# Opening of a retention-plus-FFN kernel: four overlapped steps fed by 512-byte rows, in place of four serial blocks fed by 256-byte rows

## The chip, the cores and the metric

The kernel runs on one core of a Trainium2 chip. The metric is the device time in microseconds (us) of one execution. Most figures below are medians over several executions; single executions are named as such. The time of an execution is about 1.7 us longer than the span that its profile shows.

PE is the matmul engine (TensorE), PEld its weight loads, DVE is VectorE, ACT is ScalarE, POOL is GpSimd, SP issues DMAs. A name with q (SPq) is the queue of that engine. PSUM is the memory that PE writes its results to. "FFN" is the bilinear feed-forward part.

## The reference, cut to what matters

```python
def _attn_ref(q, k, v):                      # q, k, v: float32 [8, 8, 576, 64]
    scores = scale * np.matmul(q, k.transpose(0, 1, 3, 2))
    gamma = 1.0 - 2.0 ** (-5.0 - np.arange(H))
    Dmat = np.where(rel >= 0, gamma[:, None, None] ** rel, 0.0)   # causal decay
    return np.matmul(scores * Dmat, v)

def reference(...):
    x = attn_out.transpose(0, 2, 1, 3).reshape(4608, 512)
    return (x @ w_a) * (x @ w_b) @ w_out     # 512 -> 1536 -> 512
```

The FFN is nearly all of the matmul work. The kernel computes attention for the tokens just ahead of the FFN that consumes them. At the start no token is ready, so there is an opening: the first 512 tokens go through attention before the first FFN matmul can run. Only this opening changes.

## The kernel before

The decay is split into a factor of the key's position (folded into v) and one of the query's position (a table `qs`, applied when an output is scaled). Loads of the opening are 128 tokens each, with one 256-byte row per token and head:

```python
    def load(i):
        tiles = []
        for name, src in (("qf", q), ("kf", k), ("vf", v)):
            t = half_of(stage, i, [DM], FP32, name)
            for r0, n, b, s0 in rows_of(i):
                nc.sync.dma_start(
                    t[r0:r0 + n, :].rearrange("p (h d) -> p h d", h=H),
                    src[b, :, s0:s0 + n, :].rearrange("h s d -> s h d"))
            tiles.append(t)
        staged[i] = tiles
```

The opening is four blocks of 128 tokens in order, each one cast, transposed, scored, masked, multiplied with v and the running state, and scaled. `warm` issues filler matmuls on the identity, whose results nobody reads; fourteen of them stand in the opening:

```python
    def warm(count):
        w = ps_ffn.tile([128, 4, 128], FP32, tag="ab", name="w")
        for _ in range(count):
            nc.tensor.matmul(w, identity,
                             identity.unsqueeze(1).to_broadcast([128, 4, 128]),
                             start=True, stop=True)
    ...
    idle = {0: (0, 0), 1: (0, 3), 2: (2, 4), 3: (1, 4)}
    ...
    cast(0, "dve")
    transposes(0)
    ...
    for i in range(4):
        if idle[i][0]:
            warm(idle[i][0])
        scores(i)
        flush()                      # the masks, on DVE
        if i == 2:
            load_w(0, W1)            # FFN weights, issued from POOL
            load_w(W1, W2)
        if i < 3:
            cast(i + 1, "dve" if i == 2 else "act")
        state(i)
        if idle[i][1]:
            warm(idle[i][1])
        if i < 3:
            transposes(i + 1)
            outputs(i)
            flush()                  # the scaling, on DVE
    ...
    outputs(3, halves=True)
    flush()
```

## Time and profile before

| kernel before | value |
|---|---|
| median of 3 runs | 336.48 us (336.28 to 336.54) |
| span of the profiled run | 335.1 us |
| PE busy | 95% |
| first FFN matmul | 21.74 us |

These are lines of the page of the kernel before: busy time of each engine, the DMA queues, the engines' shares in the chain of work that ended last, and one group of FFN matmuls (count, busy us, mean ns of one).

```profile
PE 318.8 (95%) x3422; PEld 165.8 (49%) x3458; DVE 164.4 (49%) x307; ACT 124.7 (37%) x261; POOL 112.4 (34%) x139
...
q1 hardware_dynamic: 147440, 45.10, 69.1%
...
PE 92%; DVE 2%; DMA 2%; issue 1%; SPq 1%; ACT 1%; POOL 0%; ACTq 0%; DVEq 0%
...
L607 PE MATMUL pb<-xT,wb_sb 128*128 128x512 bf16 (+1 forms) x474 | 111.1, 357 | 0.5
```

PE is what the kernel waits for nearly everywhere, so the place to win something is where PE has no useful work: before 21.74 us. The chain of work in order of time (start, us, what) shows why the opening is as long as it is:

```profile
4.02 5.11 DMA kf<-in_k_dram
9.13 0.05 issue
9.18 0.62 POOL qkb L254
...
12.12 1.28 PE w L651 x3
13.40 0.85 PE tp L269 x8
...
16.16 1.29 DVE sT L322 x2
17.45 0.34 DVE qkb L252
...
19.79 0.86 PE w L651 x4
20.65 0.34 PE o L341 x8
20.99 0.24 PE o L349 x8
21.24 0.02 issue
21.26 0.44 DVE xT L356
21.70 0.04 issue
21.74 0.38 PE pa L592
```

First comes a wait for a load (until 9.13 us), then PE itself, fillers included, then masks and scalings on DVE between short PE batches. `tp` are transposes, `sT` the masked scores, `o` the outputs, `xT` the scaled outputs that the FFN reads, `w` the fillers, `pa` the first FFN matmul.

The clock is part of this. The trace holds a record of each stretch with its granted clock. In the kernel before the first record, a grant of the full clock, comes at 15.2 us. Ahead of it the clock is at half, as the chain above shows: three fillers take 1.28 us at 12.12 us (0.43 us each), and four take 0.86 us at 19.79 us (0.215 us each). From then on it is full to the end. One thing has to be known of the mean clock that each run lists: a stretch ahead of the first record does not count in it, so this run is listed at 1.0 in spite of 15 us at half clock.

### The profile page before, as it was taken

How to read it: one execution, taken by the hardware profiler on the slowest of the kernel's cores; microseconds unless marked ns; L12 is line 12 of the kernel's file. 1: busy time of each engine (PE TensorE's matmuls, PEld its weight loads, DVE VectorE, ACT ScalarE, POOL GpSimd, SP SyncE). 2: the span in 40 equal slices, each digit the busy share in tenths (PEclk: the TensorE clock that was granted, in tenths of full speed). 3: DMA queues.
4: the chain of work that ended last, by engine and by line, in shares of the span. 5: the costliest groups of instructions: out<-in, count | busy, mean ns of one | idle time of the engine just before them, and what ended most of it. 6: DMA issues, size and time to landing. Idle time of an engine off the chain costs nothing.

```text
span 335.1 us, 8277 instructions
## 1 busy us (share of the span) xinstructions
PE 318.8 (95%) x3422; PEld 165.8 (49%) x3458; DVE 164.4 (49%) x307; ACT 124.7 (37%) x261; POOL 112.4 (34%) x139
## 2 busy tenths in 40 slices
PE   2989999999999999999999999999999999999995
PEld 1544445857744454545454545454545454444443
DVE  3546346565746366476237623753475347414321
ACT  8544423442624343253225232523342334213321
POOL 4570016952428638375243603370330000000000
PEclk9999999999999999999999999999999999999999
DMA  9999999989999999999599249974960420020002
GB/s 169 210 179 208 210 197 210 252 199 216 172 176 226 200 209 246 205 185 184 147 225 196 65 138 196 184 118 128 216 99 3 125 65 2 3 94 31 0 33 94
DMA packets 152230, 50.35 MB, mean 150 GB/s; under 512 B 142848, under 2 KB 147712, under 8 KB 152192
## 3 DMA queue, kind: packets, MB, share of 16 engines
q1 hardware_dynamic: 147440, 45.10, 69.1%
q0 software_dynamic: 4752, 4.72, 8.8%
q8 instruction: 27, 0.44, 0.6%
q14 instruction: 11, 0.09, 0.1%
HBM read 37.75 MB, written 9.44 MB: 141 GB/s over the span
## 4 chain that ended last, share of the span: by engine, by line
PE 92%; DVE 2%; DMA 2%; issue 1%; SPq 1%; ACT 1%; POOL 0%; ACTq 0%; DVEq 0%
PE pa L592 28%; PE pb L607 28%; PE po L627 27%; DMA kf<-in_k_dram 2%; PE o L525 2%; PE o L538 1%; PE sc L499 1%; PE kv L448 1%; SPq L121 1%; PE w L651 1%; PE tp L269 1%; DVE sT L322 1%; PE sc L316 1%; PE o L349 1%; PE o L341 0%
## 5 line engine op out<-in xcount | busy, mean ns | idle before, releaser
L612 DVE TENSOR_TENSOR hT<-ha,pb 128x512 bf16<-128x512 bf16 (+1 forms) x120 | 75.8, 633 | 98.4 <-PE pb L607 86.8
L600 ACT CAST ha<-pa 128x512 bf16<-128x512 f32 (+1 forms) x120 | 65.0, 543 | 126.6 <-PE pa L592 124.8
L592 PE MATMUL pa<-xT,wa_sb 128*128 128x512 bf16 (+1 forms) x464 | 109.5, 357 | 2.7 <-DVE xT L356 1.1
L607 PE MATMUL pb<-xT,wb_sb 128*128 128x512 bf16 (+1 forms) x474 | 111.1, 357 | 0.5
L627 PE MATMUL po<-wo_sb,hT 128*128 128x512 bf16 (+1 forms) x430 | 95.2, 373 | 1.6 <-issue 1.3
L607 PEld LDWEIGHTS <-wb_sb 128*128 128x128 bf16 x480 | 46.9, 98 | 47.6 <-issue 1.1
L592 PEld LDWEIGHTS <-wa_sb 128*128 128x128 bf16 x480 | 45.9, 98 | 47.6 <-issue 2.4
L627 PEld LDWEIGHTS <-hT 128*128 128x128 bf16 x444 | 42.4, 98 | 47.0
L388 POOL CAST qkb<-qf 64x1024 bf16<-64x1024 f32 x15 | 15.4, 1030 | 84.0 <-DMA qf<-in_q_dram 71.5
L638 DVE COPY osb<-po 128x512 f32<-128x512 f32 (+1 forms) x18 | 12.2, 676 | 43.2 <-PE po L627 43.2
L393 POOL TENSOR_TENSOR vb<-vf,vs 128x1024 bf16<-128x1024 f32 x15 | 28.5, 1902 | 7.3 <-PE o L538 2.1
L636 ACT COPY osb<-po 128x512 f32<-128x512 f32 (+1 forms) x19 | 10.9, 575 | 49.0 <-PE po L627 46.1
L547 DVE TENSOR_TENSOR xT<-o,qs 128x512 bf16<-128x512 f32 x30 | 19.6, 681 | 5.3 <-PE o L538 5.3
L467 DVE TENSOR_TENSOR sums<-kv,sums 128x256 f32<-128x256 f32 x47 | 19.8, 422 | 4.6 <-PE kv L448 3.1
L508 DVE TENSOR_TENSOR sT<-sc,mask 128x512 bf16<-128x512 f32 x30 | 19.7, 679 | 0.0
L388 POOL CAST qkb<-kf 64x1024 bf16<-64x1024 f32 x15 | 15.5, 1034 | 7.2 <-DMA kf<-in_k_dram 6.8
L392 POOL CAST qkb<-kf 64x512 bf16<-64x512 f32 x30 | 17.6, 614 | 0.9
L392 POOL CAST qkb<-qf 64x512 bf16<-64x512 f32 x30 | 17.6, 614 | 0.6
L479 ACT CAST states<-sums 64x512 bf16<-64x512 f32 (+1 forms) x30 | 17.2, 574 | 0.4
L255 POOL TENSOR_TENSOR vb<-vf,vs 128x512 bf16<-128x512 f32 x6 | 6.3, 1047 | 30.1 <-DMA vf<-in_v_dram 30.1
L269 PE MATMUL tp<-identity,qkb 128*128 128x128 bf16 x48 | 5.6, 265 | 6.4 <-ACT qkb L250 5.4
L322 DVE TENSOR_TENSOR sT<-sc,mask 128x512 bf16<-128x512 f32 x12 | 7.7, 685 | 2.4 <-PE sc L316 2.4
(71 smaller groups left out, 142.9 us busy)
## 6 DMA issues: line engine op xcount, KB each, us to landing
out_dram<-osb SPq DMA_DIRECT2D x35, 256.0 KB, 2.2
qf<-in_q_dram SPq DMA_DIRECT2D x32, 256.0 KB, 4.9
kf<-in_k_dram SPq DMA_DIRECT2D x32, 256.0 KB, 5.3
vf<-in_v_dram SPq DMA_DIRECT2D x32, 256.0 KB, 5.0
wo_sb<-in_moe_w_out_dram POOLq DMA_DIRECT2D x3, 512.0 KB, 18.3
qf<-in_q_dram SPq DMA_DIRECT2D x8, 128.0 KB, 5.1
kf<-in_k_dram SPq DMA_DIRECT2D x8, 128.0 KB, 5.5
vf<-in_v_dram SPq DMA_DIRECT2D x8, 128.0 KB, 4.8
```

The source lines that it names most:

```text
L388: nc.gpsimd.tensor_copy(qkb[0:64, w], t[0:64])
L392: nc.gpsimd.tensor_copy(to[:, :, 1 - r], fro[:, :, r])
L393: nc.gpsimd.tensor_tensor(vb.rearrange("p (k h d) -> p k h d", k=2, h=H), vf.rearrange("p (k h d) -> p k h d", k=2, h=H), vs2[:, n % BL].u ...
L467: nc.vector.tensor_tensor(sums[:, i], own, prev, op=ALU.add)
L479: nc.scalar.copy(into[half(1 - r)].rearrange("p (k a) c d -> p a k (c d)", a=2)[:, 1, which.start // 2: which.stop // 2], sums[half(r)].re ...
L508: nc.vector.tensor_tensor(sT[:, on].rearrange("p c k s -> p (c k) s"), sc[:, on].rearrange("p c k s -> p (c k) s"), mask3.unsqueeze(1).to_ ...
L547: nc.vector.tensor_tensor(x_of(t0, 128).rearrange("p c (a s) -> p c a s", a=2), o[:, :, :, kp].rearrange("p a c s -> p c a s"), qs[:, :, s ...
L592: nc.tensor.matmul(pa[:, 0:n], wa_sb[:, c, fs], xT[:, c], start=(c == 0), stop=(c == NC - 1))
L600: nc.scalar.copy(ha[:, 0:n], pa[:, 0:n])
L607: nc.tensor.matmul(pb[:, 0:n], wb_sb[:, c, fs], xT[:, c], start=(c == 0), stop=(c == NC - 1))
L612: nc.vector.tensor_tensor(hT[:, F, 0:n], has[F][:, 0:n], pb[:, 0:n], op=ALU.mult)
L627: nc.tensor.matmul(po[:, 0:width], hT[:, F, u * 128:(u + 1) * 128], wo_sb[:, F, cols], start=(F == 0), stop=(F == NF - 1))
```

## The change

The intent: load rows that are 512 bytes long (two neighbouring tokens of one head lie side by side in memory), which makes even and odd tokens two interleaved halves ("parity order"); cut the opening into four steps of 256 tokens by four heads instead of four blocks of 128 tokens by eight heads; and place each step's casts, transposes and scores ahead of the outputs of the step in front, so that the engines overlap. The core of the diff:

```diff
+    def load_step(n, hh, which):
+        ...
+        nc.sync.dma_start(
+            paired[n][which][:, hh * DM:(hh + 1) * DM]
+            .rearrange("p (h e) -> p h e", h=4),
+            (q, k, v)[which][0, 4 * hh:4 * hh + 4, 256 * n:256 * n + 256, :]
+            .rearrange("h (p two) d -> p h (two d)", two=2))
+
+    STEPS = [(0, 0), (1, 0), (0, 1), (1, 1)]
...    cut: score_step, state_step and output_step, in 64x64 quarters of PE
-    idle = {0: (0, 0), 1: (0, 3), 2: (2, 4), 3: (1, 4)}
...
+    warm(3)
+    score_step(0)
+    transpose_step(1, 0, "act")
+    transpose_step(1, 1, "act")
+    ...
+    cast_step(2, 1, "pool")
+    warm(2)
+    state_step(0, (0, 1))
+    score_step(1)
+    cast_step(2, 0, "act")
+    output_step(0)
+    state_step(1, (0,))
+    transpose_step(2, 0, "act")
+    transpose_step(2, 1, "dve")
+    load_w(0, W1)
+    output_step(1)
+    ...
+    score_step(2)
+    ...
+    transpose_step(3, 0, "act")
+    transpose_step(3, 1, "act")
+    state_step(2, (0, 1))
+    ...
+    score_step(3)
+    output_step(2)
+    state_step(3, (0,))
+    output_step(3)
+    for i in (1, 3):
+        state_step(i, (1,))
```

Five fillers are left of fourteen. The first FFN block stores its rows in two DMAs (even and odd tokens), and the query table of 768 columns is made again during that block in the usual token order.

## The prediction

> What bounds it now. The page gives PE 95% busy over the 335.1 us span; the chain that ended last is 92% PE, nearly all feed-forward (FFN) matmuls, which the change leaves alone. Only the opening is at stake. In the critical chain the first FFN matmuls that need the second half of the opening's outputs start at 22.17 us; from there to the end (313 us) I expect no change. Before them the chain is first loads (the second block's keys land at 9.13 us), then PE work at the cold clock (12 to 15.7 us), then scores, mask, output, scaling in series: mask 1.29 us for two instructions, scaling 0.69, PE batches 0.4.
>
> Loads. The q/k/v loads use 256-byte packets. The trace's packets show 217 GB/s from 2 to 16.4 us: one per 18.9 ns on each of 16 engines, 1.2 us for a 256 KB load. The weights (float32 read, bf16 written) show 206 GB/s written, so 412 GB/s read: the engines can do more. The Trainium skill ("DMA: Bandwidth & Descriptors", Specifications) puts line rate at 512 bytes or more; this trace has no such load yet. Estimate from both rates: 0.65 to 0.85 us per 256 KB load, so the loads end near 12 us instead of 16.4, and weights are issued near 10 us instead of 15.0. DMA stops being what the opening waits for.
>
> What then bounds it: ScalarE and the score, mask, output ping-pong. ScalarE carries four exponentials (914 ns for 640 columns, so about 0.75 for 512) until 5.9 us, ahead of its first transpose copy; then copies and casts of 0.59 to 0.61 us and state copies of 0.27 to 0.37. VectorE: four masks of about 1.3, four scalings of 0.69, casts and copies of 0.42. Walking both queues in order with these durations (estimates): first scores 7.3 us (before 7.15; three cold fillers stand ahead of them), mask 0 until 9.2, mask 1 11.7, scaling 0 12.4, scaling 1 13.7, mask 2 15.0, last transpose copy on ScalarE 15.3, mask 3 17.2, scaling 2 17.9, output 3 waits for that (one PSUM buffer), scaling 3 19.1. FFN matmuls of the second half then start at 19.2, against 22.17: 3.0 us saved.
>
> Costs added: total bytes are the same; the first block's stores split in two (hidden); ScalarE makes tables of 768 instead of 128 columns during the first FFN block (3 us more on an engine 37% busy, hidden); some 120 more small matmuls, in the opening's idle time.
>
> Predicted: 336.5 - 3.0 = 333.4 us, 80% range 331.6 to 335.2. Faster by over 2% 0.05, within 2% 0.94, slower 0.01.
>
> What would show each step: 512-byte packets at 300 to 400 GB/s and loads done by about 12 us; the first full FFN matmuls near 19 us; ScalarE nearly without gaps from 9 to 16 us; more PE idle in the opening; FFN from its start to the end still 313 us.
>
> What could make it wrong. The clock: the Trainium skill ("TensorE: Matmul & The Clock Gate", Part 1) says the array runs at half rate until a window of sustained activity; the trace agrees (four transposes take 0.61 us before 15.5 us, 0.40 after). The change has five fillers instead of fourteen; if FFN starts cold, up to 1.7 us come back. Weights issued early may slow the last loads (1 us). If 512-byte packets are no faster, the gain shrinks to 2 us. If copies overlap better than I walked them, up to 4.5 us are saved.

## The result

| | median | lowest to highest | runs |
|---|---|---|---|
| before | 336.51 us | 336.28 to 336.75 | 4 |
| after | 335.26 us | 334.64 to 668.54 | 4 |

The ratio is 0.9957 (95% interval 0.9937 to 0.9976). Ratios here are the mean time of one kernel's fast runs over that of the other's of the same rounds, so not quite the ratio of the medians. The three fast runs of after are 334.64, 335.10 and 335.43 us. The fourth, the profiled one, took 668.54 us, twice as long. It is a slow run and does not enter the ratio; it does enter the listed median.

The predicted 333.4 us was too low, and the listed median of 335.26 lies just outside the predicted range (331.6 to 335.2). The median of the three fast runs alone, 335.10, lies just inside it. But they save about 1.5 us where 3.1 were forecast, so less than half.

The first page of after is of that slow run. Its busy times and the group that answers to the FFN group above:

```profile
PE 648.1 (97%) x3545; PEld 247.6 (37%) x3581; DVE 166.9 (25%) x303; ACT 129.7 (19%) x271; POOL 113.1 (17%) x146
...
L768 PE MATMUL pb<-xT,wb_sb 128*128 128x512 bf16 (+1 forms) x474 | 224.0, 632 | 1.8 <-issue 1.8
```

DVE, ACT and POOL are busy for about as long as before; only PE is slower, and its three groups of FFN matmuls in about the same proportion (each is busy for 2.0 to 2.1 times as long). Its trace holds no clock record at all: the full clock was never granted in 667 us (below it is called the stuck run). This is not what the change does to a normal run, but it says where to look.

A second run of the same kernel (after_again, below) gave a profile 332.6 us long and with the clock granted at 9.5 us and then never taken back. It answers to the page of before:

```profile
PE 317.5 (95%) x3545; PEld 165.5 (50%) x3581; DVE 165.7 (50%) x303; ACT 128.9 (39%) x271; POOL 113.6 (34%) x146
...
q1 hardware_dynamic: 141360, 45.10, 66.6%
...
PE 93%; DVE 3%; issue 2%; ACT 2%; ACTq 0%; DVEq 0%
...
L768 PE MATMUL pb<-xT,wb_sb 128*128 128x512 bf16 (+1 forms) x474 | 111.1, 357 | 0.5
```

The FFN group is the same to the last digit shown, and there are 6,080 fewer packets for the same bytes. The chain of that run in its opening:

```profile
4.77 1.03 PE tp L323 x8
5.80 1.28 PE w L817 x3
7.08 0.57 PE sc L338 x14
...
9.48 0.52 PE kv L366 x16
10.02 0.37 ACT state_after L375
...
12.54 0.59 ACT qkT L325
13.12 1.04 ACT qkb L310 x2
...
15.76 1.10 DVE sT L346
16.90 0.70 DVE xT L406
17.65 0.53 PE o L390 x4
18.18 0.35 PE o L399 x16
18.53 0.62 PE kv L366 x32
19.15 0.16 issue
19.31 2.54 PE pa L753 x11
```

The DMA wait is gone from this part of the chain; it is now PE, ACT and DVE in turn, and the FFN starts at 19.31 us instead of 21.74, or 0.2 us earlier still: the trace lacks the record of the first matmul of this tile. The first FFN tile leaves PSUM 2.64 us earlier than before (ACT's copy of it ends at 20.75 against 23.38 us), and the span is 2.49 us shorter (332.60 against 335.08). This run took 334.30 us, 2.2 us less than the median before. It is also the fastest of all 15 fast runs of the changed kernel, so it shows what the change can give and not what a usual run gives. The question is why most runs do not get that.

### The profile page after: what moved, and what is told of

It is laid out like the page before. It is cut to its first block, busy times and chain, and to the rows that moved or that the text cites. A ratio compares the mean times of both kernels' runs of the same rounds, so it can differ in the third digit from the quotient of the medians.

```text
span 666.8 us, 8538 instructions
## 1 busy us (share of the span) xinstructions
PE 648.1 (97%) x3545; PEld 247.6 (37%) x3581; DVE 166.9 (25%) x303; ACT 129.7 (19%) x271; POOL 113.1 (17%) x146
## 4 chain that ended last, share of the span: by engine, by line
PE 96%; issue 1%; DMA 1%; ACT 0%; SPq 0%; DVE 0%; POOL 0%; POOLq 0%; ACTq 0%
PE pb L768 30%; PE po L788 30%; PE pa L753 30%; PE o L700 1%; PE sc L661 1%; PE o L687 1%; PE kv L610 1%; DMA vf<-in_v_dram 1%; PE kv L366 0%; PE tp L440 0%; SPq L154 0%; PE tp L572 0%; PE o L399 0%; PE tp L323 0%; PE o L390 0%
## 5 line engine op out<-in xcount | busy, mean ns | idle before, releaser
L768 PE MATMUL pb<-xT,wb_sb 128*128 128x512 bf16 (+1 forms) x474 | 224.0, 632 | 1.8 <-issue 1.8
L753 PE MATMUL pa<-xT,wa_sb 128*128 128x512 bf16 (+1 forms) x464 | 219.1, 630 | 3.6 <-issue 3.4
L788 PE MATMUL po<-wo_sb,hT 128*128 128x512 bf16 (+1 forms) x430 | 201.5, 666 | 3.3 <-issue 3.3
L768 PEld LDWEIGHTS <-wb_sb 128*128 128x128 bf16 x480 | 70.9, 148 | 130.7 <-issue 120.8
L753 PEld LDWEIGHTS <-wa_sb 128*128 128x128 bf16 x480 | 69.7, 147 | 124.2 <-issue 117.0
L788 PEld LDWEIGHTS <-hT 128*128 128x128 bf16 x444 | 63.8, 146 | 126.2 <-issue 122.6
L670 DVE TENSOR_TENSOR sT<-sc,mask 128x512 bf16<-128x512 f32 x30 | 19.7, 680 | 0.0
L641 ACT CAST states<-sums 64x512 bf16<-64x512 f32 (+1 forms) x30 | 17.2, 574 | 0.5
L661 PE MATMUL sc<-qkT 64*64 64x64 bf16 x480 | 12.3, 233 | 0.0
L700 PE MATMUL o<-sT,vb 64*64 64x64 bf16 x480 | 11.2, 228 | 0.9 <-ACT fence L728 0.9
L687 PEld LDWEIGHTS <-states 64*64 64x64 bf16 x432 | 6.6, 130 | 13.2 <-issue 13.2
```

Source lines behind the costliest of these rows:

```text
L661: nc.tensor.matmul(sc[half(a), on, c, kp, :], qkT[half(on), 1, kp, c, half(a)], qkT[half(on), 0, kp, c, half(a)], start=begun.first(on, a) ...
L670: nc.vector.tensor_tensor(sT[:, on].rearrange("p c k s -> p (c k) s"), sc[:, on].rearrange("p c k s -> p (c k) s"), mask3.unsqueeze(1).to_ ...
L753: nc.tensor.matmul(pa[:, 0:n], wa_sb[:, c, fs], xT[:, c], start=(c == 0), stop=(c == NC - 1))
L768: nc.tensor.matmul(pb[:, 0:n], wb_sb[:, c, fs], xT[:, c], start=(c == 0), stop=(c == NC - 1))
L788: nc.tensor.matmul(po[:, 0:width], hT[:, F, u * 128:(u + 1) * 128], wo_sb[:, F, cols], start=(F == 0), stop=(F == NF - 1))
```

## The experiments

Theory (clock): the opening is as short as planned where the clock is full, but it gives PE too little to do; the clock is taken back for some 3.4 us, or granted late, in most runs, and the gain shrinks. Rival (chain): the opening is simply longer than planned, because its loads or its score chain are. A second rival, that the spread comes from waits later in the FFN, is named in the expectation of after_front; no run tests it alone. All runs gave correct results except one that is wrong. "Granted clock" of a run is the mean that each run lists.

### after_again: the changed kernel once more

> The changed kernel once more, for its spread and a profile in the fast state. Clock theory: in the profiled slow run the trace holds no clock record at all and every FFN matmul takes twice as long, so the half clock was never released; fast runs should show the release late, after 17 us or inside the FFN, and some runs of 660 to 670 us may return. Timing 334.6 to 335.5 us in fast runs. Chain theory (rival): the clock is released about as in before (15 us) and the opening is long because loads and the score chain are: first FFN matmul of the second half at 20.5 to 21 us with a full clock.

Measured: 334.30, 334.48, 335.25, 335.51, 336.29 and 336.77 us, ratio to before 0.9961. Two runs are listed with a granted clock of 0.995, one with 0.999. A mean lower by 0.005 over a 333 us span is about 3.4 us at half clock, which loses 1.7 us of full-speed work. The grant was at 9.5 us in the profiled run, earlier than either theory expected: the clock theory, of a grant after 17 us, failed in this trace. The FFN start at 19.31 us contradicts the chain theory's 20.5 to 21. The spread of the slower runs was not explained yet. It is not all of the clock: the run of 336.77 us is listed at 0.999, and the kernel before had runs of 338.44 and 339.10 us at 0.999 beside it.

### before_5fill: the kernel before with five fillers

```diff
-    idle = {0: (0, 0), 1: (0, 3), 2: (2, 4), 3: (1, 4)}
+    idle = {0: (0, 0), 1: (0, 3), 2: (2, 0), 3: (0, 0)}
```

> The kernel before with five filler matmuls instead of fourteen, as the changed kernel has. Clock theory: the release comes later, the time rises by 0.5 to 2 us, and stuck runs (about 660 us) may appear. Chain theory: the fillers only fill idle time, so 336.5 us within 0.4, and no stuck run.

Measured: 337.73, 338.05, 339.61 and 342.75 us, ratio 1.0076, the last two with a granted clock of 0.995 and 0.983. No stuck run. The profiled run had its clock granted at 15.3 us as before and its first FFN tile at the same time as before (0.09 us earlier), so there the fillers left out cost nothing; that run lost 1.5 us much later, in a wait of PE at 87 us. The other full-clock run, of 337.73 us, has no trace. The wait recurs at 84 to 88 us: PE stands still there for 1.40 us in this trace, 0.89 us in that of after_nofill and 0.24 us in that of after_again, and hardly at all in that of the kernel before. PE waits for nothing that the profile shows; what it is stays open. The two runs with a lower clock speak for the clock theory: 0.017 of 341 us is 11.6 us at half clock, 5.8 us lost, and that run is 5.0 us slower than the fastest.

### after_fill: fifteen fillers in the changed kernel

```diff
-    warm(2)
+    warm(3)
     state_step(0, (0, 1))
     score_step(1)
+    warm(3)
...
     score_step(2)
+    warm(2)
...
     score_step(3)
+    warm(2)
     output_step(2)
     state_step(3, (0,))
+    warm(2)
```

> The changed kernel with fifteen fillers instead of five, in places where the trace shows PE waiting. Clock theory: the release comes earlier, no stuck runs, 333 to 334.3 us. Chain theory: nothing gained, 335 to 336.5 us, as fillers at the cold clock (0.43 us each) delay the chain.

Measured: 334.65 to 335.39 us in six runs, median 334.94, ratio 0.9941, every run with a granted clock of 1.0. The spread shrank as the clock theory said, but the level did not reach 333 to 334.3: the first FFN tile came 0.9 us later than in the fast profile of the changed kernel. Part of that is argued from the trace: the third filler ahead of the states takes 0.43 us at half clock, and the grant came 1.2 us later (10.6 us). Both theories had half of it.

### after_256: the changed kernel with 256-byte packets

```diff
-        nc.sync.dma_start(... "h (p two) d -> p h (two d)" ...)
+        for two in (0, 1):
+            nc.sync.dma_start(... "h (p two) d -> p h two d" ...[:, :, two])
```

> The changed kernel with each load issued as two of 256-byte packets, same layout and order. If the 512-byte packets are what shortened the opening: 291 GB/s falls to about 217, loads end near 16 us instead of 13, time up by 1.5 to 3 us, to 336.5 to 338. If loads are off the path: 335 us within 0.4.

Measured: 339.17 to 341.24 us, ratio 1.0098. Read from the trace's packets, the loads ran at about 220 GB/s ahead of the weights and ended at 19.4 us, as the weights came in between; the changed kernel's ran at about 290 GB/s and ended at 13.5 us. The edit also doubles the number of DMA issues, from 12 to 24. That is not what slows it: the last was issued by 14.2 us, five us before the last packet, and the kernel before, with 12 issues of 256-byte packets, has the same rate (217 GB/s). This run also lost its clock, which raises the time beyond the 338 us expected: every run is at 0.990 or lower. The windows of its trace, each one of the clock's stretches (us, busy time and instructions of the engines, PEclk, DMA share, GB/s):

```profile
11.61:15.02 3.41, 3.04 (x88) 2.08 (x81) 2.70 (x4) 2.61 (x6) 2.14 (x3) 1.00 1.34 220
15.02:18.44 3.42, 1.19 (x20) 0.79 (x20) 1.37 (x2) 1.69 (x3) 1.63 (x4) 1.00 1.32 200
18.44:21.85 3.41, 2.55 (x58) 1.79 (x59) 2.02 (x3) 1.25 (x4) 3.41 (x6) 0.50 1.13 159
```

PE waited for loads in the second window, and the clock was at half in the next two, until 25.3 us. So the larger packets are needed, and in this trace a late load also cost the clock.

### after_front: fillers ahead of everything, and six late ones

```diff
+    warm(5)
     transpose_step(0, 0, "act")
...    and the six of after_late, below
```

> The changed kernel with five fillers ahead of the first transposes, where PE is idle until 4.8 us, and six late ones in PE's idle gaps from 13 to 18 us. Clock theory (in full clock the changed opening saves its 2.6 us, and slower runs are those in which the clock came late or dropped for a 3.4 us window): release before 9.8 us, no clock loss after it, all runs 333.5 to 334.6 us. If the spread of the changed kernel comes from loads later in the FFN, it stays: 334.3 to 336.8.

Measured: 334.35, 334.41, 334.52, 334.67, 335.45 and 336.05 us, ratio 0.9941; the last two at a granted clock of 0.995. The grant came at 6.2 us in the profile. An earlier grant gained nothing at the FFN's start (0.5 us later than in the fast profile of the changed kernel) and, even with the six late fillers, did not keep the clock in two of six runs.

### after_nofill: no fillers

```diff
-    warm(3)
...
-    warm(2)
```

> The changed kernel without any filler. Clock theory: release later or dropped again, mean granted clock below 0.995 in most runs, 336 to 341 us or a run stuck at half clock. If fillers only delay the chain: 334 us, as the first scores come 0.5 us sooner.

Measured: 335.99, 336.36, 337.72 and 338.39 us, ratio 1.0006: the whole gain is gone. Two of four are at 0.995. In the profiled run the grant came at 15.1 us instead of 9.5. The first scores came 0.5 us sooner (6.53 against 7.02 us), as the rival expected, but at half clock until 15.1 us this was lost again: the first FFN tile came 1.5 us later. It was still 1.15 us ahead of the kernel before; almost 1 us of that went in the wait near 86 us described under before_5fill, which is not the clock. The run is listed at 1.0, so a late grant does not show in the listed mean. The five fillers are worth more than the time that they take.

### after_late: six fillers in the late gaps

```diff
     score_step(2)
+    warm(2)
...
     score_step(3)
+    warm(2)
     output_step(2)
     state_step(3, (0,))
+    warm(2)
```

> The changed kernel with its five fillers and six more, only between 13 and 18 us in PE's idle gaps, where they take 0.22 us each at full clock. If runs lose time because the clock drops for a window near the FFN's start: no run below 0.999, 334.3 to 335.0 us. If the loss is a late first release: no better than the changed kernel, 334.3 to 336.8.

Measured: 334.40, 334.62, 334.65 and 335.01 us, ratio 0.9934 (0.9920 to 0.9948), all at 1.0. This is what the clock theory expected of a loss near the FFN's start. The first FFN tile came 0.4 us later than in the fast profile of the changed kernel (0.5 us in that of after_late2 below), so the fillers may not be quite free.

### before_front: an earlier grant in the kernel before

```diff
     cast(0, "dve")
+    warm(5)
     transposes(0)
```

> The kernel before with five fillers ahead of its first transposes, in idle PE time. If part of the change's gain is that the clock is released at 9.8 us instead of 15.5: release here near 7 to 12 us, the PE-bound stretch from 11 to 15.5 us runs at full clock, 335 to 336 us. If the gain is of the rearranged loads and steps alone: 336.5 us within 0.3.

Measured: 336.51 to 338.60 us, ratio 1.0012: no gain. The grant came at 5.8 us in the profile, was taken back at 9.2 us, and came again at 16.0 us, later than without these fillers; the first FFN tile was 1.55 us later than before. So this kernel cannot say what an early grant that lasts would be worth; that question stays open. In this trace the grant was lost after a window in which PE was busy for 1.59 of 3.41 us.

### after_late2 and after_again2: the changed kernel with and without the six late fillers, on one chip

> The changed kernel with the six late fillers again, beside the changed kernel on one chip. If they hold the clock: 334.4 to 335.0 us in every run, mean granted clock never below 0.999. If the first four runs were luck: one or two of six at 0.995 and 335.5 to 336.8 us, as in the changed kernel.

> The changed kernel on the same chip: 334.3 to 336.8 us, at least one of six runs with a granted clock of 0.995 or lower, and perhaps one at about 668 us with the clock never released (1 of 10 so far).

Measured: with the late fillers 334.21, 334.51, 334.64, 334.86, 335.01 and 335.76 us (median 334.75, ratio to before 0.9917); without them 335.44, 335.54, 335.83, 335.92, 335.94 and 337.94 us (median 335.88, ratio 0.9952). Five of the six without them have a granted clock of 0.995 or lower, one of the six with them. The mean of the one six over that of the other is 0.9962, so the late fillers are worth 1.3 us here. By its own words the expectation of after_late2 was missed: one run at 0.995 and 335.76 us is what it gave for luck. What speaks for the fillers is the kernel without them on the same chip, with five of six. (On this chip most runs of the kernel before took 338 us.) No stuck run came back.

The profile of after_again2 fell on the slowest run and shows what happens. Its page has the drop in the row of the granted clock, in the second and third of 40 slices:

```profile
PEclk9779999999999999999999999999999999999999
```

Its windows, cut at the clock records, and below them those of the fast run after_again:

```profile
9.25:12.67 3.42, 2.56 (x71) 1.69 (x70) 1.75 (x3) 1.66 (x5) 3.19 (x6) 1.00 1.15 291
12.67:16.08 3.41, 3.41 (x60) 2.85 (x58) 2.23 (x4) 2.71 (x7) 2.96 (x6) 0.50 1.00 144
16.08:19.49 3.41, 2.46 (x84) 1.77 (x80) 2.43 (x4) 1.68 (x5) 3.41 (x5) 1.00 1.30 202
19.49:22.91 3.42, 3.09 (x53) 1.83 (x43) 0.69 (x1) 1.35 (x5) 3.13 (x10) 0.50 1.24 207
22.91:26.32 3.41, 3.41 (x18) 1.51 (x17) 0.69 (x1) 1.44 (x3) 0.86 (x2) 1.00 1.20 207
```

```profile
9.47:12.88 3.41, 2.92 (x87) 2.16 (x90) 2.24 (x3) 2.22 (x6) 3.18 (x5) 1.00 1.16 286
12.88:16.29 3.41, 2.71 (x74) 1.80 (x74) 2.94 (x5) 3.09 (x7) 2.83 (x6) 1.00 1.18 152
16.29:19.70 3.41, 2.87 (x88) 2.11 (x88) 2.00 (x3) 1.24 (x5) 3.41 (x5) 1.00 1.26 198
```

The second number after the window is PE's busy time, and the third value from the end is PEclk. In the slow run two windows in which PE was busy for 2.56 and 2.46 us were each followed by one at half clock, the second of them at the FFN's start; in the fast run the windows have 2.71 to 2.92 us and the clock stays. The same instructions stand in both. The differences that the traces show ahead of the first drop are a window that falls 0.2 us earlier and a v load that landed 0.7 us later (8.70 against 7.96 us). These are the windows of after_late2, with the six late fillers in the last two:

```profile
8.45:11.86 3.41, 2.53 (x64) 1.58 (x63) 2.04 (x2) 2.43 (x5) 3.09 (x6) 1.00 1.15 292
11.86:15.27 3.41, 3.41 (x78) 2.50 (x77) 2.85 (x5) 2.65 (x7) 2.95 (x5) 1.00 1.05 176
15.27:18.68 3.41, 3.12 (x75) 1.90 (x74) 2.43 (x4) 1.71 (x6) 3.41 (x6) 1.00 1.30 203
```

The late fillers raise PE's busy time in the later windows. They come after the first window and cannot hold the clock there; it kept the clock with 2.53 us here. The chain of the slow run at the FFN's start:

```profile
18.95 0.38 PE o L390 x4
19.34 0.41 PE o L399 x16
19.74 1.01 PE kv L366 x32
20.75 0.32 issue
21.07 3.45 PE pa L753 x11
```

Against the fast run the 32 state matmuls take 1.01 us instead of 0.62, and the first FFN matmuls 3.45 us instead of 2.54. Not all of the 3.6 us between the two spans is clock: about 0.7 us were lost ahead of the first drop, with the late v load; about 2.0 us between that drop and the end of the second window at half clock; and 0.8 us in a wait of PE for a cast on DVE at 53 us.

What exactly is watched? PE's busy share does not sort the windows: windows of 2.24 and 2.21 us busy (before_5fill) and of 2.53 us (after_late2) kept the clock, and one of 2.56 us lost it. Another sum sorts better: moving columns (the columns that a matmul streams through the array) times the used part of the 128x128 array, each matmul counted by the share of its time that falls in the window. A window full of FFN matmuls (512 columns every 0.2155 us) would have about 8,100. The four windows after which the clock dropped, in all traces of fast runs, have 1,085, 2,055, 2,592 and 2,738. Of the 35 others that began between a grant and the first FFN matmul, 34 have 2,784 or more, and one of 2,648 kept the clock. The windows at half clock sort at about the same place: all 17 before a grant have 2,859 or more, and of the 32 others 31 have 2,675 or less and one 2,975. This is a fit, chosen after the fact: counted by where a matmul starts, a window of 2,944 lost the clock and one of 2,560 kept it, and the stuck run does not obey it at all (below). If it holds, it would explain why the change is so exposed, as its small products run in 64x64 quarters, and each counts for a quarter; no run tests that.

### before_512: only the larger packets, in the kernel before

```diff
+            if i < 4:
+                nc.sync.dma_start(
+                    t.rearrange("p (h e) -> p h e", h=4),
+                    src[0, 4 * (i % 2):4 * (i % 2) + 4,
+                        256 * (i // 2):256 * (i // 2) + 256, :]
+                    .rearrange("h (p two) d -> p h (two d)", two=2))
+                tiles.append(t)
+                continue
```

> The kernel before with its first twelve loads in 512-byte packets (four heads of two tokens per partition, so its output is wrong on purpose; the amounts, shapes and order of all work stay). If the loads alone make the change's gain: loads at 290 GB/s, FFN start 2 us earlier, 334 to 335 us. If the steps' overlap is needed as well: the opening is still bound by PE at half clock and the score chain, 335.3 to 336.5 us; a gain below 1.2 us.

Measured: 335.49 to 335.91 us in four runs, all at a clock of 0.999 or 1.0. The first FFN tile came 1.17 us earlier than before, with the clock granted at 12.7 us. The gain is below 1.2 us, as was expected if the steps' overlap is needed too. (Its output is wrong, which doesn't matter for the time. The ratio to before, 0.9941, is against that chip's slower runs of before, so the trace is the better measure.) So the loads alone give a little under half of the 2.64 us; the steps are needed for the rest. Notable is how steady it is: with nine more fillers and larger products on PE it holds its clock, and its median of 335.74 us is no worse than that of the changed kernel beside it.

### after_hold: two more fillers

```diff
     score_step(1)
+    warm(2)
...    and the six of after_late
```

> The six late fillers and two more between the second scores and the first output, where PE waits 0.5 us for the states at about 11 us. A trace of the changed kernel showed the clock dropped after the windows 9.6 to 13.0 and 16.4 to 19.8 us. If both windows must be kept busy: no run of six below 0.999, 334.3 to 335.0 us, and the one outlier of ten with the late fillers alone (335.76 us at 0.995) does not return. If the two only delay the chain: 334.9 to 335.4 us, as with fifteen fillers.

Measured: 334.18, 334.28, 334.52, 334.69, 335.01 and 336.53 us, median 334.61, ratio 0.9949; none below 0.999. (The drops that the expectation refers to followed the windows from 9.3 and 16.1 us.) The two fillers cost nothing at the FFN's start and no listed clock is low, but the outlier did not go away, which the expectation had excluded: 336.53 us at a listed clock of 1.0. A grant that comes one window later would look like that, as it does not count in the listed mean, but no trace shows that run. It is not clearly better than after_late.

The best version is the changed kernel with the six late fillers: 334.65 us median over ten runs on two chips, against 335.51 us over the 15 fast runs of the changed kernel, and ratios to before of 0.9934 and 0.9917. Only one of these chips ran both kernels; there the medians are 334.75 and 335.88 us.

## Why the prediction was wrong

1. **Right: what the chain would be.** The walk through ACT's and DVE's queues held in the fast profile. Mask 1 was predicted to end at 11.7 us and ended at 11.6; mask 2 at 15.0 and 15.1; mask 3 at 17.2 and 17.0; scaling 3 at 19.1 and 19.3.
2. **Right in direction, a little off in size: the loads.** Predicted 0.65 to 0.85 us for 256 KB and an end near 12 us; measured 0.9 us (about 290 GB/s) and 13.5 us. It cost nothing in the fast profile, as the chain was elsewhere; in that of after_again2 a late v load did stand in the chain. The packets do matter: after_256 lost all of the gain, and before_512 won 1.17 us with them alone. The Trainium skill ("DMA: Bandwidth & Descriptors", Specifications) gives 512 bytes as the least size for line rate. The traces agree that 512 is much better than 256 (290 against 217 GB/s), but not that it is line rate: the weights' reads went at about 412 GB/s in the trace of before, in packets of 768 to 1,280 bytes as written (the rate is twice that of the bf16 bytes written, as they are cast from float32).
3. **Also failed, by about half a us: the FFN's start.** The prediction put the extra small matmuls "in the opening's idle time". In the fast profile 32 state matmuls (0.62 us in the chain) and the two FFN matmuls of the first half stand between the last outputs and the first FFN matmul of the second half, and scaling 3 hides only part of them. The first matmul that needs the second half started at 19.53 us against 22.17, so the saving at the FFN was 2.64 us instead of 3.0, and 2.49 us in the span.
4. **The step that failed: "if FFN starts cold, up to 1.7 us come back".** This was named as a risk and given no part of the central value; that was the wrong weight. Of the 15 fast runs of the changed kernel, seven have a listed clock of 0.995 or lower, and their median is 335.92 us; that of the other eight is 335.18. after_again2's trace shows two drops, the second over the FFN's first 1.8 us; six late fillers moved the median on the same chip from 335.88 to 334.75 us and the runs at 0.995 or lower from five of six to one, with nothing else changed. So a loss of clock is shown as a cause of the missing time in the changed kernel. It is not shown for the three fast runs that the prediction was compared with: 334.64, 335.10 and 335.43 us are all listed at 1.0 and have no trace. A late grant, which that mean does not count, or a later wait in the FFN would fit them, and neither was tested.
5. **Also failed: the reasoning about where the clock would be decided.** The prediction counted fillers, five instead of fourteen. In the traces the clock changes at the ends of stretches of 3.41 us, so what counts is where the fillers stand: with five before 9.5 us the grant came at 9.5 us, without them at 15.1 us, and then there are none for the ten us in which it has to be held.
6. **Right: the costs that were called hidden.** Tables and split stores left no mark; the FFN groups have the same mean times, and from the first FFN tile to the last ACT's copies in the two traces keep their distance within 0.5 us.

Left open: the stuck run (1 of 16 runs of the changed kernel, none of the 48 of before and none of the 28 with more fillers). In it PE was busy for 97% of 667 us, and its FFN matmuls make about 3,700 of the columns counted above per 3.4 us even at half clock, more than 11 of the 17 windows before a grant elsewhere; too little activity by this count does not explain that it was never granted. Open too are four runs of 335.1 to 335.5 us with a listed clock of 1.0, which a late grant would explain but no trace shows, and the waits near 53 and 86 us, which cost up to 0.8 and 1.4 us in single traces and may be part of the spread.

## What to carry to other kernels

When a change makes a stretch of a PE-bound kernel leaner, check what the clock does in that stretch in several traces, window by window, not in one: a single profile can show the full gain (2.2 us here) while the median run has lost half of it. Try fillers in PE's gaps through the whole stretch up to the dense part, and not only at its start: here the six late ones won 1.3 us on average on one chip, though the first FFN tile came 0.4 to 0.5 us later in their traces than in the fastest without them. And compare a load's packet size with the rate that larger packets reach in the same trace before deciding that the DMA is at its limit.

## What the Trainium skill lacked or had wrong

- "TensorE: Matmul & The Clock Gate", Part 1, ties the fall to half clock to an idle window of about 3.4 us, and its rule is no PE-idle gaps of over about 3.4 us. It also tells of a kernel whose clock swung because PE paused briefly but often. The window's length agrees (the stretches are 3.41 us long), and so do falls without a long gap: the clock fell after windows in which PE was busy for 2.56 and 2.46 of 3.41 us and no two matmul starts were more than 0.73 us apart. The page lacks a measure of how much activity keeps the clock. No sure one comes out of these runs either; the count of columns above sorts all but one of 39 windows near 2,750, a third of a dense one.
- The same page says that the grant comes after one sustained busy window. One run had PE busy for 97% of 667 us and never got it. The page's caveat tells of a clock stuck at a quarter for over 50 us, not of one at half for a whole execution.
- "TensorEngine Tiling (Array Packing)" tells the gain of packing small products into quarters; it does not say how such products count towards the clock. In the count above each counts for a quarter; no run tests it alone.
- "DMA: Bandwidth & Descriptors", Specifications: 512 bytes is given as the least size for line rate. Loads of 512-byte rows ran at about 290 GB/s here, against about 400 GB/s of reads for the longer rows of the weights in the same trace (200 GB/s written).
